# Infini-attention and GEGLU on one core: the hand-ordered main path replaced by one that a list scheduler orders at build time

## The chip, the cores and the metric

The kernel runs on one core of a Trainium2 chip. The metric is the device time of one execution in microseconds, as the median of several runs. The core has TensorE (PE, matrix multiplication), VectorE (DVE), ScalarE (ACT), GpSimd (POOL) and SyncE (SP, which issues most transfers). Each engine works through its own instructions in the order in which the program emits them, and waits for semaphores that other engines and transfers raise.

## The reference

The input is x, 2048 tokens of 448 features in bfloat16. Two branches share its layer norm, and the result is `x + s * silu(f)`.

```
xn = layernorm(x)
q, k, v = xn @ wq, xn @ wk, xn @ wv          # 16 heads of 28
for s in 4 segments of 512 tokens:            # per head
    a_dot = softmax(q k^T / sqrt(28) + causal mask) v
    a_mem = (phi(q) M) / (phi(q) z + 1e-6)    # phi(t) = t + 1 if t > 0 else exp(t)
    o     = g * a_mem + (1 - g) * a_dot       # g = sigmoid(beta)
    M, z += phi(k)^T v, sum phi(k)
s_out = o @ wo
f     = (gelu(xn @ w_gate) * (xn @ w_up)) @ w_down    # 448 -> 1792 -> 448
out   = x + s_out * silu(f)
```

## The kernel before

Work goes by segments of 512 tokens. The 448 features are cut into four chunks of 112 rows (`DC`), so that every matmul over features is four matmuls of 112 rows. The heads are padded from 28 to 32 columns and go in four groups of four, so that a group fills 128 partitions of `qT` and `kT`; column 28 of the padded v (`vaug`) is one and gives the softmax denominators.

The steps of a segment, with the lines that matter:

- **Layer norm** (L188 to L211): statistics and scaling on DVE, the power on POOL (L194), 16 transposes on PE (L204) and copies into `xnT`.
- **Projections** (`project_units`): q and k transposed, 512 columns wide (L253, casts L258 and L260), v by tokens (L275), and k once more by tokens (`ktok`, L283), from which phi(k) is formed for the memory update; phi(q) from L263 on.
- **Attention** (`attention`, `scores`, `pv`): 12 steps, three for each head group. A step has two half-steps of two heads. A half-step makes scores of two heads (L337, 32 rows each) into one of two score buffers in PSUM, exponentiates them on ACT (L341) and masks the diagonal blocks on POOL (L344). PV (L354) puts four heads into four column groups. `evac` (L364) copies the result and sends its denominators to DRAM (L366).
- **Reciprocals** (`invert`, L383 to L393): the denominators come back in another shape (`dc`), are inverted on DVE, go to DRAM (`rdr`, four transfers) and come back spread over partitions (`rb`, four transfers of 256 KB). `combine` (L408 to L411) scales on POOL and writes `oT`.
- **Memory** (`memory_read` L370, `update` L314 on).
- **Gate and up** (`gate_up`): 14 blocks of 128 columns; each has eight matmuls of 112 rows (L422), a Gelu on ACT (L425) and a product on DVE (L426). The blocks share the two score buffers in PSUM.
- **Down** (L437, 56 matmuls of 448 columns) and **finish** (L461 output projection, L464, L466 the residual on POOL, with x loaded once more as `xr`, L458).

The order is written by hand. For segments 0 to 2, gate and up of segment s come first, with tables that put layer norm, reciprocals and combining between its blocks. Attention of s follows, and `attention` fills the gaps between its half-steps with units of other work in proportion to costs written beside them: update, projections of s+1, down of s, finish of s-1. Segment 3 is the other way round: attention first, filled with down and finish of segment 2, then gate and up, then down and finish.

```
keyed.append(((c + u[0] / 2) / tot, n, u))     # merge(): units of several lists by share of cost
while fill and done < tot * n / (2 * len(steps)):   # attention(): fill after each half-step
```

Nearly all transfers are issued by SP in program order. PSUM holds two score buffers of two banks, one bank for PV and three for everything else.

Of the kernel before, what the change touches and what calls it, by code (L numbers as in the profile page):

```python
# [9 lines left out]
ALU = mybir.AluOpType  # L10
# [10 lines left out]
HG = 4  # L21
# [3 lines left out]

def fast_path(tc, A_x, A_wq, A_wk, A_wv, A_wo, A_beta, B_w_gate, B_w_up, B_w_down, out):
# [10 lines left out]
    DC = 112  # L37
    NDC = D // DC
    NFC = F // P
    RC = L // 64  # L40
    scale = float(Dh) ** -0.5

    with ExitStack() as ctx:
        pool = lambda name, bufs, **kw: ctx.enter_context(tc.tile_pool(name=name, bufs=bufs, **kw))
        const = pool("const", 1)
        xp = pool("xp", 2)
        xnp = pool("xnp", 2)
        seg1 = pool("seg1", 1)
        seg2 = pool("seg2", 2)
        work = pool("work", 2)  # L50
        ptp = pool("ptp", 6)
        oup = pool("oup", 4)
        rbp = pool("rbp", 4)
        blk = pool("blk", 5)
        small = pool("small", 4)
        dram = pool("dram", 2, space=DRAM)
        ps_s = pool("ps_s", 2, space=PSUM)
        ps_pv = pool("ps_pv", 1, space=PSUM)
        ps_m = pool("ps_m", 3, space=PSUM)
# [4 lines left out]
        def w_dma(eng, t, ap, rows):  # L64
            eng.dma_start(out=t[:], in_=ap.rearrange("(c p) n -> p c n", p=rows))

        x_sb = {}

        def load_x(s):
            x_sb[s] = xp.tile([P, NB, D], BF16, name="x_sb")  # L70
            for b in range(0, NB, 2):
                eng = nc.scalar if s == 0 and b else nc.sync
                eng.dma_start(out=x_sb[s][:, b:b + 2, :], in_=x_v[s][:, b:b + 2, :])

        load_x(0)
        ident = const.tile([P, P], BF16, name="ident")
        make_identity(nc, ident[:])
        nhalf = const.tile([P, NB], F32, name="nhalf")
        nc.gpsimd.memset(nhalf[:], -0.5)
        warm = const.tile([P, 1], F32, name="warm")  # L80
        nc.scalar.activation(out=warm[:], in_=nhalf[:, 0:1], func=ACT.Exp)

        wq_raw = seg2.tile([DC, NDC, D], BF16, name="oT")
        wk_raw = const.tile([DC, NDC, D], BF16, name="wk_raw")
        wv_sb = const.tile([DC, NDC, D], BF16, name="wv_sb")
        wg_sb = const.tile([DC, NDC, F], BF16, name="wg_sb")
        wu_sb = const.tile([DC, NDC, F], BF16, name="wu_sb")
        wd_sb = const.tile([P, NFC, D], BF16, name="wd_sb")
        wo_sb = const.tile([P, G, D], BF16, name="wo_sb")
        w_dma(nc.sync, wq_raw, A_wq, DC)  # L90
        w_dma(nc.scalar, wk_raw, A_wk, DC)
        w_dma(nc.sync, wv_sb, A_wv, DC)
        betac = const.tile([P, 1], A_beta.dtype, name="betac")
        nc.gpsimd.dma_start(
            out=betac[:],
            in_=A_beta.rearrange("(h o) -> h o", o=1).unsqueeze(1).to_broadcast([H, RC, 1]))
        w_dma(nc.sync, wg_sb, B_w_gate, DC)
        w_dma(nc.scalar, wu_sb, B_w_up, DC)
        load_x(1)
        w_dma(nc.sync, wd_sb, B_w_down, P)  # L100
        nc.gpsimd.memset(wo_sb[:], 0.0)
        wo_v = A_wo.rearrange("(g i d) n -> i d g n", i=HG, d=Dh)
        for i in range(HG):
            nc.sync.dma_start(out=wo_sb[i * HP:i * HP + Dh, :, :], in_=wo_v[i])

        raw = {"wq": wq_raw, "wk": wk_raw}
        wpad = {}
        for nm in ("wq", "wk"):
            wpad[nm] = const.tile([DC, NDC, H, HP], BF16, name=nm + "_pad")
            nc.gpsimd.memset(wpad[nm][:, :, :, Dh:HP], 0.0)  # L110

        def pad_weight(nm):
            nc.vector.tensor_copy(out=wpad[nm][:, :, :, 0:Dh],
                                  in_=raw[nm][:].rearrange("p c (h d) -> p c h d", d=Dh))

        bdmask = const.tile([P, P], F32, name="bdmask")
        vaug, pkb = [], []
        macc = const.tile([P, G, P], F32, name="macc")
        mbd = const.tile([P, G, P], BF16, name="mbd")
        igate = const.tile([P, 2], F32, name="igate")  # L120
        for i in range(2):
            vaug.append(const.tile([P, NB, H, HP], BF16, name=f"vaug{i}"))
            nc.gpsimd.memset(vaug[i][:, :, :, Dh:HP], 0.0)
            nc.gpsimd.memset(vaug[i][:, :, :, Dh:Dh + 1], 1.0)
        pkb.append(const.tile([P, NB, H, HP], BF16, name="pkb"))
        nc.gpsimd.memset(pkb[0][:, :, :, Dh:HP], 0.0)
        nc.gpsimd.memset(bdmask[:], 0.0)
        for i in range(HG):
            nc.gpsimd.memset(bdmask[i * HP:(i + 1) * HP, i * HP:(i + 1) * HP], 1.0)

        def gates():

            nc.scalar.activation(out=igate[:, 0:1], in_=betac[:], func=ACT.Exp)
            nc.scalar.activation(out=igate[:, 1:2], in_=betac[:], func=ACT.Exp, scale=-1.0)
            nc.vector.tensor_scalar(out=igate[:], in0=igate[:], scalar1=1.0, scalar2=2.0,
                                    op0=ALU.add, op1=ALU.mult)


        clock, waiting = [0], []

        def later(n, fn):
            waiting.append((clock[0] + n, len(waiting), fn))

        def tick():
            clock[0] += 1
            due = sorted(w for w in waiting if w[0] <= clock[0])
            waiting[:] = [w for w in waiting if w[0] > clock[0]]
            for _, _, fn in due:
                fn()

        oki = const.tile([1, 1], mybir.dt.int32, name="oki")

        def guard():
            sqs = {}
            for i, nm in enumerate(("wq", "wk")):
                sqs[nm] = oup.tile([DC, NDC, D], BF16, name=f"oU{i}")
                nc.scalar.activation(out=sqs[nm][:], in_=raw[nm][:], func=ACT.Square)
            ones = const.tile([P, 1], BF16, name="ones")
            nc.gpsimd.memset(ones[:], 1.0)
            nrm = small.tile([1, 2, H], F32, name="nrm")  # L160
            yield
            for i, nm in enumerate(("wq", "wk")):
                np_ = ps_m.tile([P, L], F32, name="m")
                for c in range(NDC):
                    nc.tensor.matmul(out=np_[0:1, 0:D], lhsT=ones[0:DC, :], rhs=sqs[nm][:, c, :],
                                     start=(c == 0), stop=(c == NDC - 1))
                nc.vector.reduce_sum(out=nrm[:, i, :],
                                     in_=np_[0:1, 0:D].rearrange("p (h d) -> p h d", d=Dh), axis=AX.X)
            okh = small.tile([1, H], F32, name="okh")
            nc.vector.tensor_tensor(out=okh[:], in0=nrm[:, 0, :], in1=nrm[:, 1, :], op=ALU.mult)  # L170
            nc.vector.tensor_scalar(out=okh[:], in0=okh[:], scalar1=(LOGIT_MAX / (D * scale)) ** 2,
                                    scalar2=None, op0=ALU.is_lt)
            nc.vector.tensor_reduce(out=oki[:], in_=okh[:], op=ALU.min, axis=AX.X)
            yield

        xnT = {}

        def layer_norm(s):

            xs = x_sb[s]  # L180
            xnT[s] = xnp.tile([DC, NDC, L], BF16, name="xnT")
# [782 lines left out]
```

## Time and profile before

| what | value |
| --- | --- |
| time, median of 3 runs | 335.21 us (335.02 to 335.26) |
| profiled execution, from first to last instruction | span 331.6 us |
| its own time outside the span | not recorded apart; the median is 3.6 us above the span |
| PE busy | 279.2 us, 84%, 1620 matmuls |
| DVE, ACT, POOL busy | 159.5, 152.0, 132.9 us |
| mean granted TensorE clock | 0.951 |
| read from and written to memory | 17.66 MB and 2.98 MB |
| instructions | 4480 |

A line of the profile names the line of the kernel, the engine, the operation, the tile that is written and those that are read, their shapes, the count, the busy time, the mean length of one, and the idle time of the engine ahead of it with what ended it. Busy time of PE is the union of matmuls that overlap in its pipeline, so a cost on PE is read from the distance between starts.

### The profile page before, as it was taken

To read this page: it belongs to the slowest core of one execution; us is meant where nothing else is said; L and a number is where in the kernel's file an instruction comes from. 1 tells how busy PE (TensorE), PEld (TensorE's weight loads), DVE (VectorE), ACT (ScalarE), POOL (GpSimd) and SP (SyncE) were. 2 spreads that over 40 slices of the span, in tenths; PEclk is the share of its full clock that TensorE was granted. 3 is DMA by queue.
4 is the path that set the end of the run, shared out by engine and by line. 5 is a ranking of instruction groups with operands and counts; after the bars stand their busy time and mean duration, and the time that the engine had idled before them with its cause. 6 is when DMAs were issued, how large, how long until landed. Compare 5 with 4: busy or idle time off the path is not lost.

```text
span 331.6 us, 4480 instructions
## 1 busy us (share of the span) xinstructions
PE 279.2 (84%) x1620; PEld 116.1 (35%) x1620; DVE 159.5 (48%) x301; ACT 152.0 (46%) x213; POOL 132.9 (40%) x219
## 2 busy tenths in 40 slices
PE   0699989999999999989999998198837973979691
PEld 0344434433334434333444432022312321434250
DVE  2447746645559567655585576145202531233221
ACT  1324542867772355556733386246643650223010
POOL 7000100333311245459410983286546743216712
PEclk9999999999999999999999999659996997799898
DMA  6998000000000520340102300510050021514011
GB/s 199 267 265 211 0 1 2 0 2 4 0 3 5 144 56 21 85 102 29 33 6 70 74 8 18 155 43 29 22 135 9 8 59 57 143 22 140 0 55 51
DMA packets 20773, 21.00 MB, mean 63 GB/s; under 512 B 6424, under 2 KB 16152, under 8 KB 20744
## 3 DMA queue, kind: packets, MB, share of 16 engines
q1 hardware_dynamic: 19512, 18.41, 21.3%
q10 hardware_dynamic: 1200, 2.24, 2.5%
q8 instruction: 14, 0.23, 0.3%
q14 instruction: 15, 0.12, 0.1%
q0 software_dynamic: 32, 0.00, 0.0%
HBM read 17.66 MB, written 2.98 MB: 62 GB/s over the span
## 4 chain that ended last, share of the span: by engine, by line
PE 54%; DMA 16%; POOL 11%; SPq 6%; DVE 5%; ACT 3%; issue 3%; POOLq 0%; DVEq 0%; ACTq 0%
PE s L422 21%; PE m L253 8%; PE m L437 7%; DMA xr<-in_A_x_dram 6%; PE s L337 5%; PE m L275 3%; DMA rdr<-dc 3%; POOL o_out L466 3%; POOL oU L410 3%; PE pv L354 3%; POOL oT L411 3%; PE m L283 3%; SPq L390 2%; SPq L393 2%; DMA oT<-in_A_wq_dram 2%
## 5 line engine op out<-in xcount | busy, mean ns | idle before, releaser
L341 ACT ACTIVATE pt<-s 128x1024 bf16<-128x1024 f32 (+1 forms) x96 | 81.6, 883 | 45.3 <-PE s L337 33.7
L344 POOL TENSOR_SCALAR_AFFINE_SELECT pt<-pt 128x256 bf16<-128x256 bf16 x128 | 51.7, 424 | 66.8 <-ACT pt L341 63.8
L425 ACT ACTIVATE gl<-s 128x512 bf16<-128x512 f32 x56 | 33.3, 597 | 75.1 <-PE s L422 75.0
L422 PE MATMUL s<-xnT,wg_sb 112*128 112x512 bf16 x224 | 58.9, 386 | 3.3 <-DVE hT L426 3.3
L426 DVE TENSOR_TENSOR hT<-gl,s 128x512 bf16<-128x512 bf16 x56 | 38.1, 683 | 49.2 <-ACT gl L425 49.1
L422 PE MATMUL s<-xnT,wu_sb 112*128 112x512 bf16 x224 | 58.4, 384 | 0.0
L437 PE MATMUL m<-wd_sb,hT 128*128 128x448 bf16 x224 | 51.8, 368 | 0.0
L354 PE MATMUL pv<-pt,vaug 128*32 128x512 bf16 (+3 forms) x256 | 21.2, 324 | 24.6 <-POOL pt L344 17.0
L337 PE MATMUL s<-qT,kT 32*128 32x128 bf16 (+3 forms) x256 | 33.1, 309 | 2.5 <-ACT pt L341 2.3
L466 POOL TENSOR_TENSOR o_out<-sg,xr 128x448 bf16<-128x448 f32 x16 | 16.9, 1059 | 41.0 <-DMA xr<-in_A_x_dram 31.4
L422 PEld LDWEIGHTS <-wu_sb 112*128 112x128 bf16 x224 | 22.1, 99 | 27.1 <-issue 1.3
L422 PEld LDWEIGHTS <-wg_sb 112*128 112x128 bf16 x224 | 21.1, 99 | 27.6 <-issue 6.4
L437 PEld LDWEIGHTS <-hT 128*128 128x128 bf16 x224 | 20.4, 101 | 22.6 <-issue 6.8
L194 POOL TENSOR_TENSOR rstd<-rstd,nhalf 128x2 f32<-128x2 f32 x8 | 5.8, 727 | 48.2 <-DVE rstd L192 48.1
L364 DVE COPY oU<-pv 128x512 f32<-128x512 f32 x16 | 11.0, 686 | 25.5 <-PE pv L354 15.3
L410 POOL TENSOR_TENSOR oU<-oU,rb 128x512 f32<-128x512 f32 x12 | 15.2, 1266 | 19.6 <-DMA rb<-rdr 19.6
L337 PEld LDWEIGHTS <-kT 32*128 32x128 bf16 x256 | 9.9, 92 | 37.2 <-issue 36.5
L446 DVE SCALAR_TENSOR_TENSOR sg<-th,m 128x448 f32<-128x448 f32 x16 | 9.9, 619 | 26.6 <-ACT th L441 24.4
L253 PE MATMUL m<-xnT,wq_pad 112*128 112x512 bf16 x64 | 19.1, 427 | 0.7 <-ACT xnT L209 0.7
L354 PEld LDWEIGHTS <-vaug 128*32 128x32 bf16 x256 | 6.5, 94 | 37.4 <-issue 34.2
L253 PE MATMUL m<-xnT,wk_pad 112*128 112x512 bf16 x64 | 18.6, 418 | 0.0
L461 PE MATMUL m<-wo_sb,oT 128*128 128x448 bf16 x64 | 16.0, 369 | 3.0 <-POOL oT L411 3.0
(76 smaller groups left out, 275.3 us busy)
## 6 DMA issues: line engine op xcount, KB each, us to landing
rb<-rdr SPq DMA_DIRECT2D x28, 256.0 KB
xr<-in_A_x_dram SPq DMA_DIRECT2D x16, 112.0 KB
out_dram<-o_out SPq DMA_DIRECT2D x16, 112.0 KB
x_sb<-in_A_x_dram SPq DMA_DIRECT2D x7, 224.0 KB
wu_sb<-in_B_w_up_dram ACTq DMA_DIRECT2D x1, 1568.0 KB
wg_sb<-in_B_w_gate_dram SPq DMA_DIRECT2D x1, 1568.0 KB
wd_sb<-in_B_w_down_dram SPq DMA_DIRECT2D x1, 1568.0 KB
rdr<-dc SPq DMA_DIRECT2D x28, 32.0 KB
```

The lines of the kernel that those rows point to most:

```text
L253: nc.tensor.matmul(out=pr[:], lhsT=wpad[nm][:, c, g * HG:(g + 1) * HG, :].rearrange("p h d -> p (h d)"), rhs=xnT[s][:, c, :], start=(c == ...
L337: nc.tensor.matmul(out=sp[:, j, c0:c0 + n], lhsT=kT[s][r, g, kb * P:(kb + 1) * P], rhs=qT[s][r, g, kb * P:L], start=True, stop=True)
L341: nc.scalar.activation(out=pt[:, :, 0:w], in_=sp[:, :, 0:w], func=ACT.Exp, scale=scale)
L344: nc.gpsimd.affine_select(out=v, in_=v, pattern=[[0, 2], [1, P]], compare_op=ALU.is_ge, fill=0.0, base=0, channel_multiplier=-1)
L354: nc.tensor.matmul(out=acc[i * HP:(i + 1) * HP, kb * P:L], lhsT=va[:, kb, g * HG + i, :], rhs=pts[i // 2][:, i % 2, c0:c0 + n], start=(kb ...
L410: nc.gpsimd.tensor_tensor(out=o_a[:], in0=o_a[:], in1=r[:], op=ALU.mult)
L422: nc.tensor.matmul(out=gu[:, i, :], lhsT=w_sb[:, c, fc * P:(fc + 1) * P], rhs=xnT[s][:, c, :], start=(c == 0), stop=(c == NDC - 1))
L425: nc.scalar.activation(out=gl[:], in_=gu[:, 0, :], func=ACT.Gelu_apprx_tanh)
L426: nc.vector.tensor_tensor(out=hT[s][:, fc, :], in0=gl[:], in1=gu[:, 1, :], op=ALU.mult)
L437: nc.tensor.matmul(out=d_ps[:, 0:D], lhsT=hT[s][:, fc, b * P:(b + 1) * P], rhs=wd_sb[:, fc, :], start=(fc == 0), stop=(fc == NFC - 1))
L461: nc.tensor.matmul(out=a_ps[:, 0:D], lhsT=oT[s][:, g, b * P:(b + 1) * P], rhs=wo_sb[:, g, :], start=(g == 0), stop=(g == G - 1))
L466: nc.gpsimd.tensor_tensor(out=o_out[:], in0=t[:], in1=xr[:], op=ALU.add)
```

## The change

The whole main path is written anew. Every piece of work becomes an `Op` with engine, an assumed occupation and latency, dependences, buffers and a priority; `arrange` goes through them with a list scheduler while the program is built, and the ops are emitted in the order of the start times that it assigns. What runs is still a fixed order on each engine with semaphores.

What else differs: attention has ten steps per segment instead of twelve, each with all four heads of a group, and with the short key blocks of two groups packed together; one step fills both score buffers. The 448 features are cut into three chunks of 128 rows and a remainder of 64. For gate and up, the remainders of gate (partitions 0 to 63) and up (64 to 127) lie in one tile, `wh_sb`, and are issued as neighbours for two blocks; the last chunk of `xnT` holds its 64 rows twice. Projections still take four matmuls, the remainder padded with zeros. `xnT` of segments 1 to 3 and phi(k) by tokens come from DMA transposes; k by tokens is no longer computed. x stays in SBUF for all four segments. phi works on two groups at a time, its min and max on POOL. Attention comes ahead of gate and up in every segment. PSUM has two score buffers and four other banks, which gate and up may use as well.

The diff, cut to its core ("-" lines are the code above and are left out):

```diff
+SEM, SWITCH, TABLE, AHEAD = 0.06, 0.1, 1.29, 0.2
+def arrange(ops):
...
+        t0, _, e0, _, _ = min(found, key=lambda c: c[:2])
+        s, _, e, o, picks = min((c for c in found if c[2] == e0 and c[0] <= t0 + AHEAD),
+                                key=lambda c: c[1])
+        occ, lat = o.eng[e]
+        if e == "PE" and o.mode and o.mode != mode:
+            s, mode = s + SWITCH, o.mode
...
+        o.start, o.on, o.done = s, e, s + lat
+        free[e] = s + occ
...
+    return sorted(done, key=lambda o: o.start)
...
+        S_ = banks(2, [P, 2, L], "s")
+        M_ = banks(4, [P, L], "m")
...
+        def dma(name, kb, fn, **kw):
+            return op(name, {"SP": (0.42, 2.0 + kb / 180)}, fn, **kw)
...
+        def warm_up():
+            for i in range(12):
+                nc.tensor.matmul(out=M_.aps[3], lhsT=warm[:, 0:P], rhs=warm[:], start=True, stop=True)
...
@@ layer_norm, s > 0 @@
+                for b in range(NB):
+                    o = dma(f"tr{s}{b}", 128, lambda b=b: nc.sync.dma_start_transpose(
+                        out=xT.ap()[:, :, b * P:(b + 1) * P], in_=xn.ap()[:, b, :]),
...
@@ phi @@
+                o = act(f"ex{nm}{s}{half}", 2 * L, lambda: nc.scalar.activation(
+                    out=e.ap(), in_=src[0].ap()[:, gs, :], func=ACT.Exp), func="exp",
...
+                o = gps(f"mi{nm}{s}{half}", 1.0, lambda: nc.gpsimd.tensor_scalar(
+                    out=e.ap(), in0=e.ap(), scalar1=1.0, scalar2=0.0, op0=ALU.min, op1=ALU.max),
...
+                        pk[s][1].append(dma(f"tk{s}{g}", 128, lambda j=j, g=g:
+                            nc.sync.dma_start_transpose(out=dst.ap()[:, g], in_=e.ap()[:, j, :]),
...
+        def steps_of(g0, g1):
+            return [[(g0, 0, 0)], [(g0, 1, 0), (g0, 3, 384)], [(g0, 2, 0), (g1, 2, 256)],
+                    [(g1, 0, 0)], [(g1, 1, 0), (g1, 3, 384)]]
...
@@ attention, scores of one step @@
+                    for g, kb, c0 in st:
+                        n = L - kb * P
+                        for i in range(HG):
+                            r = slice(i * HP, (i + 1) * HP)
+                            nc.tensor.matmul(out=S2[i // 2].ap()[:, i % 2, c0:c0 + n],
+                                             lhsT=kT[s][0].ap()[r, g, kb * P:(kb + 1) * P],
+                                             rhs=qT[s][0].ap()[r, g, kb * P:L], start=True, stop=True)
...
+                for pr in range(2):
+                    x = act(f"ex{s}{k}{pr}", 2 * L, lambda pr=pr: nc.scalar.activation(
+                        out=pt.ap()[:, 2 * pr:2 * pr + 2, :], in_=S2[pr].ap(), func=ACT.Exp,
...
@@ gate_up, two blocks @@
+                def halves(fc=fc, bank=bank):
+                    for j in range(2):
+                        for i in range(2):
+                            r = slice(i * HALF, (i + 1) * HALF)
+                            nc.tensor.matmul(out=bank(j, i), lhsT=wh_sb[r, (fc + j) * P:(fc + j + 1) * P],
+                                             rhs=xT.ap()[r, NC3, :], start=True, stop=False)
...
+        for s in range(NSEG):
+            if s == 0:
+                layer_norm(1, at(A(0), -100))
+            attention(s, A(s))
+            if s > 0:
+                read(s, at(A(s), 0))
+            if s < LAST:
+                update(s, at(A(s), 10))
...
+            gate_up(s, Gp(s), tabled)
+            tabled = []
+            combine(s, at(Gp(s), -500))
...
+            if s + 2 <= LAST:
+                layer_norm(s + 2, at(Gp(s), 100))
...
+        for b in range(NB):
+            down(LAST, b, at(8, 10 * b))
+            finish(LAST, b, at(8, 10 * b + 5))
...
+        with tc.manual_schedule():
+            for o in arrange(ops):
+                if o.fn is not None:
+                    o.fn()
```

More of the change, by code (lines that the diff above doesn't have):

```diff
@@ L116, in fast_path @@
[L116 to L125, printed above, removed]
```

1124 lines of the change are left out of this document (683 added, 441 removed).

## The prediction

> **What bounds the kernel now.** I read the page first: the busy tenths in 40 slices, with the granted clock below.
>
> ```profile
> PE   0699989999999999989999998198837973979691
> PEclk9999999999999999999999999659996997799898
> ```
>
> TensorE (PE) is full from the third slice to about 200 us; after that it has holes and a lowered clock. Then the stretches between stage limits, taken from the timeline: start, gate/up 0, attention 0, gate/up 1, attention 1, gate/up 2, and all after that (segment 3). Columns are length, then busy time of each engine with instruction counts, then clock and DMA.
>
> ```profile
> core 0: us, PE busy (x) PEld busy (x) DVE busy (x) ACT busy (x) POOL busy (x), PEclk, DMA share, GB/s
> 0.00:29.60 29.60, 18.19 (x81) 8.69 (x82) 12.85 (x29) 7.70 (x13) 6.80 (x23) 1.00 0.97 249
> 29.60:58.40 28.80, 27.41 (x140) 12.58 (x139) 17.35 (x39) 12.82 (x18) 1.50 (x3) 1.00 0.07 16
> 58.40:95.00 36.60, 36.60 (x252) 14.26 (x253) 20.60 (x38) 27.20 (x40) 13.35 (x33) 1.00 0.01 2
> 122.50:163.40 40.90, 39.93 (x266) 15.93 (x267) 25.04 (x44) 26.20 (x36) 23.83 (x41) 1.00 0.21 55
> 189.90:331.60 141.70, 103.43 (x598) 40.23 (x595) 49.43 (x81) 56.69 (x77) 71.75 (x105) 0.88 0.21 56
> ```
>
> Segments 0 to 2 are bound by PE: less time there needs less PE work. Segment 3 is bound by waits: PE idles 38.3 of 141.7 us. The waits view names one of them, POOL behind reloads of x:
>
> ```profile
> POOL o_out L466 <- DMA xr<-in_A_x_dram: 31.4, 10, 9.6
> ```
>
> Next, durations by shape, then PE's timeline at an ordinary attention step and at one in segment 3 (start, length, instruction, count).
>
> ```profile
> L341 ACT ACTIVATE pt<-s 128x1024 bf16<-128x1024 f32 x64 | 63.4, 1025 | 28.8 <-PE s L337 18.5 <-POOL o_out L466 8.6 <-POOL pt L344 1.7
> L344 POOL TENSOR_SCALAR_AFFINE_SELECT pt<-pt 128x256 bf16<-128x256 bf16 x128 | 51.7, 424 | 66.8 <-ACT pt L341 63.8 <-DMA den<-oU 2.5
> L283 PE MATMUL m<-wk_raw,xnT 112*128 112x448 bf16 x48 | 10.6, 354 | 0.1
> ...
> 67.30 0.39 PE L337 MATMUL s<-qT,kT 32*128 32x512 bf16 x2
> 67.61 0.40 PE L354 MATMUL pv<-pt,vaug 128*32 128x384 bf16 x8
> 67.95 1.12 PE L437 MATMUL m<-wd_sb,hT 128*128 128x448 bf16 x5
> 69.00 0.39 PE L337 MATMUL s<-qT,kT 32*128 32x512 bf16 x2
> ...
> 255.31 0.40 PE L337 MATMUL s<-qT,kT 32*128 32x512 bf16 x6
> 255.64 0.29 PE L354 MATMUL pv<-pt,vaug 128*32 128x256 bf16 x4
> ```
>
> Starts, not lengths, give the cost, since matmuls overlap. A full 512-column matmul takes 0.216 us (gate/up chunks of eight start 1.73 apart), so 0.213 is streaming; one of 448 takes 0.189. Five of 448 should take 0.945 and take 1.05 (67.95 to 69.00): leaving for a 32-row form costs 0.105. Two scores of 512 take 0.31: together 0.213, plus 0.10 for the next change of form. The six at 255.31 are 2,048 columns in 0.33 us: four 32-row groups run at once (one after another would be 0.85).
>
> **The change, part by part.** PE work of one segment, in us.
>
> *Gate/up.* Now 14 x 8 x 0.216 = 24.2. Then per two blocks: four 64-row matmuls in two pairs (2 x 0.213), 12 full ones (2.59), two changes of form (0.21) = 3.23, times 7 = 22.6. That the two 64-row groups run together no row shows. Bounds: as the 32-row groups do (22.6), or one after the other (+0.43 x 7 = 25.6). I take 22.6, the nearest row being the four-group one.
>
> *Scores and PV.* Now 24 score groups of two heads: 10,240 columns at two at once (4.3) and two changes each (5.1), and 12 PV groups (2.1 + 12 x 0.12), about 13. Then 10 steps of four heads: 10 x (0.105 + 0.213 + 0.105 + 0.213 + 0.125) = 7.6. On ACT the 24 exps (16 of 1025, 8 of 601 ns, 20.6 busy) become 20 of 1025, 19.8 at the 0.99 busy each that the row gives. The masks on POOL stay 32 x 0.424.
>
> The Trainium skill (TensorE: Matmul & The Clock Gate, Measured speedup vs the span model) measured 3.07 times for four row groups, not 4. By that the scores would stream 2.8 us a segment instead of 2.1 and the sum would be 2.6 us higher; the 0.33 us for six matmuls speaks for 4.
>
> *Removed from PE.* The token-major k matmuls, 16 x 0.189 = 3.0 in segments 0 to 2, and the 16 LayerNorm transposes of each of segments 1 to 3 (L204: 64 busy for 7.1 us, so 1.8 a segment). They become 24 DMA transposes of 128 KB on SP's queue, and phi(k) is taken from kT.
>
> *The transposes' price.* No row has one. Below: a plain load of like size, xr (112 KB), lands in 2.0 us and holds SP for 0.43; the POOL and DVE work around them is kept off PE, so no gain beyond that PE time. Above: if it went in 32-byte pieces, 4,096 packets at 58 ns each (21.3% of 16 x 331.6 us over 19,512 packets of q1) on 16 engines: 14.8 us. I take 2.5, nearest to the like-sized load. xnT is needed a whole stage later, so this is hidden; what waits behind them in SP's queue are the den, dc, rdr and rb transfers and the stores. If the cover is gone, PE stalls at the projection, and once more at update.
>
> The Trainium skill (VectorE: DVE Perf Modes, The three transpose paths) puts a 128x128 DMA transpose at 1309 ns against 390 on TensorE, which speaks against this edit; an estimate from it is 5.2 us per transpose, 42 per segment on the queue, and the sum of the third rival below. No run here shows it yet.
>
> *x kept on chip* removes 16 reloads and POOL's 31.4 us behind them; in segments 1 and 2 PE was full all the same, so the gain counts in segment 3.
>
> *The order.* Now gate/up(s) precedes attention(s). Then attention(s) comes first, with down and output projection of s-1 and projection of s+1 between its steps, then gate/up(s), and at the end only down and output projection of segment 3. So attention 3 has PE fill and the reciprocal chain (den, dc, rdr, rb, about 20 us) runs beside 22.6 us of gate/up. What it adds: one step's scores fill both score buffers, so the next step's first complete exp often waits for both exps. A row's price for that turn: scores start 240.19, exp 240.68, 0.49, against zero where the second head pair alone is late; I take 0.45.
>
> The stages then, each the larger of PE and ACT plus what their coupling loses:
>
> - Start to first exp: x lands at 4.1; four blocks of statistics, scaling and copies fill DVE for 6.5; transpose and copy 1.3; two projections 1.73; cast and scores 1.0: 14.6.
> - Attention 0: PE 7.6 + 9.9 (projection) + 1.0 (update) is less than ACT: 19.8 + 6 phi exps (6.0) + 10 x 0.45 = 30.3.
> - Attention 1: PE 7.6 + 9.9 + 10.6 (down, 56 x 0.189) + 3.0 + 1.0 + 0.9 = 33.0; ACT 19.8 + 4.0 + 2.2 (tanh) + 4.5 + 1.3 (table) = 31.8. So near each other they lose some: 36. Attention 2, two phi exps fewer: 35.5.
> - Attention 3: PE 22; ACT 19.8 + 2.2 + 4.5 + 1.3 = 27.8: 28.5.
> - Gate/up: 4 x 22.6 = 90.4. Eight handovers at 0.5: 4.
> - Down and output projection: 13.6. From PE's end: tanh, two products and a DVE add (now POOL's 1.03) 2.8, and 3.9 from the last store's issue to the end as now: 6.7.
>
> Sum: 14.6 + 130.3 + 90.4 + 4 + 13.6 + 6.7 = 259.6. The profiled span is 331.6 and the median 335.2, so 3.6 lies outside it: **263 us**. By stages, the gain is mostly segment 3's: after gate/up 2 the rest takes 142 us now, and 28.5 + 22.6 + 13.6 + 6.7, with handovers about 72, then.
>
> **Rivals.**
> - *Lock-step (0.20).* PE works in a fixed order; if it reaches the scores inside a fill block (up to 1.05), every step costs 2.0 of exp, 0.6 of other ACT work, 0.5 turn and 1.0 of late arrival: 41, 41, 36 and 33 us for the four attentions instead of 130.3, 151 in all. For: both score buffers go at once, and ACT and PE are 1 us apart. Against: today's PE is full in attention 0. Time: 284.
> - *The pairing does nothing (0.06).* The 64-row halves run one after the other, so this part of the change does not do what it says: +0.43 x 28 = 12, 275.
> - *Transposes somewhat late (0.07).* At 5 us each, between the bounds, the four before a projection take 10 us longer than forecast; the stage before hides some 6, the rest is a stall, three times: 275.
> - *Transposes very slow (0.06), slower than before.* At 14.8 us each, 24 hold SP's queue for 355 us, and everything else in it comes on top: about 370. It decides from about 7 us, where eight per segment no longer fit beside the rest of the queue in a 57 us segment, and makes the kernel slower from about 10: (335 - 263) / 24 = 3 us beyond those 7. For: 16,152 of 20,773 packets of now are under 2 KB, so small pieces do happen. Against: a plain load of the size takes 2.0.
>
> **How the numbers follow.** The forecast has 0.60 (its own range 250 to 276), the rivals 0.20, 0.06, 0.07, 0.06, and 0.01 is left for no change that can be told: about 0.2%, 0.7 us, is what a measurement of this kernel can tell. Low end: no turn and no coupling loss, attentions 26 + 33 + 33 + 24, 14 less, and half the handovers: 247. High end: lock-step with transposes a few us late, 292. Faster 0.93, same 0.01, slower 0.06.
>
> **What would show it.** Right: gate/up pairs 3.2 us apart; scores of a one-part step 0.33 apart; PE at 8 tenths or more to the last slices, clock whole; ACT's exps 2.4 us per step in attention 0; transposes landing near 2.5 us; SP's queue far from full. Wrong: ACT's idle time before L341's successor above 1 us per step (lock-step); pairs 3.7 apart (no pairing); PE waiting for xnT (transposes). The forecast falls if PE idles over 60 us in all.

## The result: 290.4 us, faster, but 27 us short of the forecast

The changed kernel takes 290.44 us (289.36 to 291.33, four runs) beside 335.12 us for the kernel before on the same chip: 0.8688 of it, 95% interval 0.8639 to 0.8737. The gain is 44.7 us where 72 was forecast. The profiled execution took 290.03 us with a span of 288.3, so 1.7 us lie outside the span, not 3.6. Medians count every execution; where some ran at a lower clock, in the second group of experiments above all, the ratio uses the others alone and so is not the quotient of the medians.

The page of the changed kernel: PE's busy tenths and clock in 40 slices of 7.2 us, then two groups (busy, mean ns, idle time ahead).

```profile
PE   7893029889997999599769999989697999998991
PEclk9996557999999999999979999999999999999998
...
L682 ACT ACTIVATE pt<-s 128x1024 bf16<-128x1024 f32 x80 | 77.5, 1022 | 34.5 <-PE s L670 33.3
...
L638 DVE TENSOR_TENSOR oa<-oa,rb 128x512 f32<-128x512 f32 x12 | 13.6, 1169 | 9.2 <-DMA rb<-rdr 9.2
```

The holes that PE had after 200 us are gone: the last half is at 9 tenths nearly throughout. There are new ones: a deep one in the fourth to sixth slice, with the clock down to half, one in the twentieth and twenty-first, and one at 5 tenths in the seventeenth (115 to 122 us, in attention 1), to which the open points come back. The windows put the first two at 20 to 50 and at 140 to 150 us (length, busy us and instructions of each engine, then granted clock, DMA share, GB/s):

```profile
core 0: us, PE busy (x) PEld busy (x) DVE busy (x) ACT busy (x) POOL busy (x), PEclk, DMA share, GB/s
20.00:30.00 10.00, 3.97 (x40) 1.23 (x37) 2.34 (x3) 7.47 (x10) 8.04 (x16) 0.68 1.13 271
30.00:40.00 10.00, 0.00 (x0) 0.00 (x0) 7.11 (x19) 0.00 (x0) 0.00 (x0) 0.50 0.60 82
40.00:50.00 10.00, 8.85 (x60) 3.76 (x60) 4.71 (x10) 3.81 (x4) 2.19 (x5) 0.63 0.18 37
140.00:150.00 10.00, 5.52 (x19) 1.69 (x18) 7.02 (x8) 1.79 (x3) 5.72 (x4) 0.83 0.32 77
```

From 30 to 40 us PE, ACT and POOL do nothing at all; only DVE works. The waits view (total us, times, longest) names what came last for each hole:

```profile
PE m L450 <- DMA xnT<-xn: 14.4, 1, 14.4
...
DVE st L365 <- DMA x_sb<-in_A_x_dram: 11.1, 2, 10.2
DVE oa L638 <- DMA rb<-rdr: 9.2, 6, 4.3
PE m L765 <- DVE hT L785: 8.0, 4, 4.5
```

Stage by stage, us. A is attention, G gate/up. G starts at its first gate/up matmul, and the next A at the first other matmul behind the last of them; the last eight PV matmuls of attentions 0 and 3 so fall into G0 and G3 of the changed kernel. The best experiment is the one with the transposes of segment 1 back on PE, below.

| | first score | A0 | G0 | A1 | G1 | A2 | G2 | A3 | G3 | down, output | tail |
|---|---|---|---|---|---|---|---|---|---|---|---|
| forecast, 0.5 of handover in each A and G | 14.6 | 30.8 | 23.1 | 36.5 | 23.1 | 36.0 | 23.1 | 29.0 | 23.1 | 13.6 | 6.7 |
| changed kernel | 15.5 | 45.7 | 24.1 | 40.3 | 29.0 | 35.6 | 25.7 | 27.4 | 25.3 | 13.8 | 6.0 |
| best experiment | 15.8 | 34.0 | 26.7 | 32.7 | 22.5 | 35.7 | 22.5 | 28.9 | 25.2 | 13.8 | 5.9 |

Against the first row A0 is 14.9 us over, A1 3.8, the four gate/ups together 11.7 and the start 0.9; down and output add 0.2, and A2, A3 and the tail give 2.7 back. That is, but for rounding, the 28.7 us by which the span is longer than the forecast sum.

### The profile page after: what moved, and what is told of

The parts are those of the page before. It is cut to its first block, busy times and chain, and to the rows that moved or that the text cites. A ratio compares the mean times of both kernels' runs of the same rounds, so it can differ in the third digit from the quotient of the medians.

```text
span 288.3 us, 4343 instructions
## 1 busy us (share of the span) xinstructions
PE 241.7 (84%) x1562; PEld 100.5 (35%) x1562; DVE 173.2 (60%) x286; ACT 147.3 (51%) x183; POOL 129.2 (45%) x210
## 5 line engine op out<-in xcount | busy, mean ns | idle before, releaser
L682 ACT ACTIVATE pt<-s 128x1024 bf16<-128x1024 f32 x80 | 77.5, 1022 | 34.5 <-PE s L670 33.3
L802 PE MATMUL m<-wd_sb,hT 128*128 128x448 bf16 x224 | 46.6, 353 | 0.5 <-DVE qT L460 0.3
L450 PE MATMUL m<-xnT,wq_pad 128*128 128x512 bf16 (+1 forms) x80 | 17.5, 349 | 14.4 <-DMA xnT<-xn 14.4
L785 DVE TENSOR_TENSOR hT<-gl,s 128x512 bf16<-128x512 bf16 x31 | 20.3, 677 | 13.3 <-ACT gl L781 13.3
L781 ACT ACTIVATE gl<-m 128x512 bf16<-128x512 f32 x25 | 14.9, 597 | 20.5 <-PE m L775 17.3
L775 PE MATMUL s<-xnT,wg_sb 128*128 128x512 bf16 x93 | 25.3, 381 | 0.0
L775 PE MATMUL s<-xnT,wu_sb 128*128 128x512 bf16 x93 | 25.1, 379 | 0.0
L670 PE MATMUL s<-qT,kT 32*128 32x512 bf16 (+3 forms) x256 | 19.4, 307 | 5.9 <-ACT pt L682 5.6
L729 PE MATMUL m<-pt,vaug 128*32 128x128 bf16 (+3 forms) x256 | 18.6, 315 | 3.6 <-POOL pt L694 3.4
L775 PE MATMUL m<-xnT,wg_sb 128*128 128x512 bf16 x75 | 21.0, 391 | 0.0
L775 PE MATMUL m<-xnT,wu_sb 128*128 128x512 bf16 x75 | 20.7, 385 | 0.0
L638 DVE TENSOR_TENSOR oa<-oa,rb 128x512 f32<-128x512 f32 x12 | 13.6, 1169 | 9.2 <-DMA rb<-rdr 9.2
L450 PE MATMUL m<-xnT,wk_pad 128*128 128x512 bf16 (+1 forms) x80 | 17.4, 348 | 0.0
```

The lines of the kernel that those rows point to most:

```text
L450: nc.tensor.matmul(out=bank.ap()[:, lo:hi], lhsT=wpad[nm][:, c, g * HG:(g + 1) * HG, :].rearrange("p h d -> p (h d)"), rhs=xT.ap()[:, c, l ...
L638: o = dve(f"ca{s}{g}", 0.6, lambda t=t, r=r: nc.vector.tensor_tensor(out=t.ap(), in0=t.ap(), in1=r.ap(), op=ALU.mult), deps=[o, ro], prio= ...
L670: nc.tensor.matmul(out=S2[i // 2].ap()[:, i % 2, c0:c0 + n], lhsT=kT[s][0].ap()[r, g, kb * P:(kb + 1) * P], rhs=qT[s][0].ap()[r, g, kb * P ...
L682: x = act(f"ex{s}{k}{pr}", 2 * L, lambda pr=pr: nc.scalar.activation(out=pt.ap()[:, 2 * pr:2 * pr + 2, :], in_=S2[pr].ap(), func=ACT.Exp, ...
L729: nc.tensor.matmul(out=acc[g].ap()[i * HP:(i + 1) * HP, kb * P:L], lhsT=va[s][0].ap()[:, kb, g * HG + i, :], rhs=pts[kk][0].ap()[:, i, c0: ...
L775: nc.tensor.matmul(out=bank(j, i), lhsT=w[:, c, (fc + j) * P:(fc + j + 1) * P], rhs=xT.ap()[:, c, :], start=False, stop=(c == NC3 - 1))
```

## The experiments

Each ran beside the kernel before on its own chip (median 334.31, 335.02 and 334.34 us in the three groups), which is what the ratios are against. In the second group (wo late, both weights late, the combine on POOL, and all of these together) the kernel before scattered from 329.78 to 335.97 us, so their intervals are wide. Since the order is made by `arrange`, an edit to an assumed time or an engine can also move other work; where that shows, it is said.

### The hole in attention 0

DVE's and SP's timelines of the changed kernel (start, length, instruction, count, idle ahead). SPq rows are SP's issues, and their length is the time that SP was held:

```profile
12.31 11.84 SPq L318 DMA_DIRECT2D wo_sb<-in_A_wo_dram  x4
24.20 0.40 SPq L320 DMA_DIRECT2D x_sb<-in_A_x_dram  x1
24.70 5.03 SPq L512 DMA_TRANSPOSE pk<-e  x2
34.64 5.12 SPq L419 DMA_TRANSPOSE xnT<-xn  x4
```

```profile
32.51 0.63 DVE L365 BATCH_NORM_STATS2 st<-x_sb 128x6 f32<-128x448 bf16 x1 [10.16 <-DMA x_sb<-in_A_x_dram]
33.05 1.30 DVE L387 TENSOR_SCALAR xn<-x_sb,mv,rs 128x448 bf16<-128x448 bf16 x4
...
41.15 1.86 PE L450 MATMUL m<-xnT,wq_pad 128*128 128x512 bf16 x4 [14.41 <-DMA xnT<-xn]
```

Read from the bottom. PE's projection of segment 1 waits for segment 1's transposes. They wait for four scalings of 0.33 us on DVE. These stand in DVE's order behind a statistic of segment **3**, which waits 10.16 us for x of segment 3. That x was issued at 24.20, because the four loads of wo ahead of it held SP for 11.84 us. The plan had 0.42 us for each of these issues and had x landing 12 us after its own. Theory: the wait goes in pieces, as x, wo and w_down are taken out of the transposes' way. Rival: the transposes themselves are slow.

**x of segment 3 loaded earlier, the plan's order kept.**

```diff
+        nc.sync.dma_start(out=xs[3][:], in_=x_v[3])      # behind x of segment 1
-        x_in[3] = [op("x3", {"SP": (0.42, 12.0)}, lambda: nc.sync.dma_start(out=xs[3][:], in_=x_v[3]),
-                      after=wo_in, prio=0)] * NB
+        x_in[3] = [op("x3", {"SP": (0.42, 12.0)}, None, after=wo_in, prio=0)] * NB
```

> The changed kernel with one transfer moved: x of segment 3 is issued right behind x of segment 1 instead of behind wo; the order on every compute engine is unchanged. Theory (DVE stands at the statistics of segment 3's x, 22.3 to 32.5 us, and the scaling of segment 1 is queued behind them): the 14.4 us wait of PE for xnT goes, and with it some 2.5 us of half clock behind it; span 288 to about 272, time about 274. Rival (the DMA transposes or the full DMA engines make xnT late): the wait stays above 8 us, because x arrives no sooner on SP's queue than the transposes leave it; time 283 to 290.

Measured: 284.98 us, ratio 0.8537 (0.8477 to 0.8597), 5.5 less than the changed kernel. DVE's wait is gone, but PE's is not. The timelines of this run:

```profile
13.57 11.65 SPq L319 DMA_DIRECT2D wo_sb<-in_A_wo_dram  x4
...
28.03 6.75 SPq L419 DMA_TRANSPOSE xnT<-xn  x4
...
36.15 0.58 PE L450 MATMUL m<-xnT,wq_pad 128*128 128x512 bf16 x1 [9.15 <-DMA xnT<-xn]
```

SP is still held by wo until 25.2, and the pair of phi(k) transposes goes first. The theory is right in part, 5.3 of the 14.4 us; the time and the 9.15 us that are left lie where the rival had put them.

**The plan told the truth about x.** The loads stay; `x3` is said to land after 27 us instead of 12, so that `arrange` puts segment 3's statistics later.

```diff
-        x_in[3] = [op("x3", {"SP": (0.42, 12.0)}, lambda: ...
+        x_in[3] = [op("x3", {"SP": (0.42, 27.0)}, lambda: ...
```

> The changed kernel with one number of the scheduler changed: it is told that x of segment 3 lands 27 us after its issue instead of 12; no transfer moves. Theory: segment 3's statistics go behind segment 1's scaling on DVE and the PE wait for xnT falls from 14.4 to under 3 us; time 273 to 278. Rival (transposes or DMA load): the wait stays, 283 to 290.

Measured: 283.83 us, ratio 0.851 (0.8458 to 0.8562): 6.6 us for one number. PE's wait for xnT is 7.9 us, not under 3, so this too ends in the rival's range. Here the order moved elsewhere too: A1 fell to 34.9 while G0 rose to 26.1.

**wo behind segment 1's transposes**, with x early:

```diff
+                wo_in[0].after += [xnT[1][1][-1], pk[0][1][-1]]
+                for n in range(1, HG):
+                    wo_in[n].after.append(wo_in[n - 1])
```

> As x3_early, and the four loads of wo are issued behind segment 1's transposes and phi(k)'s, so SP is free from about 13.5 us instead of 25.3; the order on the compute engines is the same. Theory (SP's queue, held 11.7 us by wo's four issues, makes the transposes late): the 9.15 us wait of PE that x3_early left falls to under 3 us; time about 277. Rival (the transposes wait in the DMA rings behind the weights, w_down above all, which land until about 30 us): the wait falls by under 3 us; time 282 to 285.

Measured: 280.95 us, ratio 0.8517 (0.8343 to 0.8691). PE's wait for xnT falls by 2.05 us to 7.10, not to under 3 as the theory had it; the rival had a fall of under 3.

**w_down behind them as well**: its load becomes an op, and wo follows it.

```diff
-        nc.sync.dma_start(out=wd_sb[:], in_=B_w_down.rearrange("(c p) n -> p c n", p=P))
+        wd_in = op("wd", {"SP": (0.42, 12.0)}, lambda: nc.sync.dma_start(
+            out=wd_sb[:], in_=B_w_down.rearrange("(c p) n -> p c n", p=P)), prio=0)
+                wd_in.after += [xnT[1][1][-1], pk[0][1][-1]]
+                wo_in[0].after.append(wd_in)
```

> As wo_late, and w_down too is issued behind the transposes. SP's queue alone is at fault: the same as wo_late. The rings' backlog is at fault: the wait that wo_late leaves falls here to under 2 us; time 274 to 277. Either way, if the wait goes and the time does not, the reading of attention 0 is wrong.

Measured: 280.95 us, ratio 0.8508 (0.8343 to 0.8672). The two times can't be told apart, but the traces differ: PE's wait for xnT falls from 9.15 to 7.10 with wo late and to 5.77 with w_down late too, where a backlog of the weights as the only cause would have left under 2. A0 falls from 45.7 (changed kernel) over 40.4 (x early) and 37.3 to 36.4. Neither theory held alone. With SP free and the scalings done, the last 5.8 us are the transposes' own way. In the version with both weights late and the combine on POOL (below), they look like this:

```profile
26.44 5.12 SPq L420 DMA_TRANSPOSE xnT<-xn  x4
...
32.90 1.86 PE L451 MATMUL m<-xnT,wq_pad 128*128 128x512 bf16 x4 [5.77 <-DMA xnT<-xn]
```

Four issues of 1.28 us and 1.3 to land: 6.5 us from first issue to first use. This is far cheaper than the 10 us that I took for four, but it lies on the path.

### The waits in gate/up

The hole at 140 us, in DVE's and PE's timelines of the changed kernel:

```profile
136.05 0.69 DVE L785 TENSOR_TENSOR hT<-gl,s 128x512 bf16<-128x512 bf16 x1 [0.61 <-ACT gl L781]
141.08 0.69 DVE L638 TENSOR_TENSOR oa<-oa,rb 128x512 f32<-128x512 f32 x1 [4.34 <-DMA rb<-rdr]
142.05 3.94 DVE L638 TENSOR_TENSOR oa<-oa,rb 128x512 f32<-128x512 f32 x3 [0.28 <-DMA rb<-rdr]
145.92 1.27 DVE L785 TENSOR_TENSOR hT<-gl,m 128x512 bf16<-128x512 bf16 x2
...
146.65 1.18 PE L765 MATMUL m<-xnT,wh_sb 64*128 64x512 bf16 x3 [4.48 <-DVE hT L785]
```

The combine's first product (L638, `oa` times the reciprocals in `rb`) is put on DVE by the change, and waits 4.3 us for rb. The products `hT` stand behind it although their inputs are there; PSUM banks are not freed, and PE stops for 4.48 us. The four products themselves then hold DVE until 145.99, another 4.9 us.

**The combine's first product on POOL** (segments 0 to 2).

```diff
-                    o = dve(f"ca{s}{g}", 0.6, lambda t=t, r=r: nc.vector.tensor_tensor(
+                    e, t_ = (gps, 1.27) if s < LAST else (dve, 0.6)
+                    o = e(f"ca{s}{g}", t_, lambda t=t, r=r: (nc.gpsimd if s < LAST else nc.vector).tensor_tensor(
```

> The changed kernel with the first product of combine (oa x rb) on POOL instead of DVE for segments 1 and 2; nothing else. Theory (DVE stands at these products, waiting for rb, and gate/up's products are queued behind them): PE's waits of 4.48 and 2.61 us in gate/up 1 and 2 go, with 1.5 us of half clock behind the first; gate/up 1 and 2 take 23 to 24.5 instead of 29.0 and 25.7 us, time 283 to 285. Rival (DVE has too much to do in gate/up whatever it waits for): gate/up 1 stays above 27.

Measured: 277.52 us, ratio 0.8381 (0.8209 to 0.8552): 12.9 less than the changed kernel, more than expected. G1 goes from 29.0 to 22.53 and G2 from 25.7 to 22.54, which is the forecast's PE work of 22.6; G0 and A0 give 0.9 and 1.1. The waits of this run show the same late rb, now in front of an engine on which nothing urgent is queued:

```profile
POOL oa L639 <- DMA rb<-rdr: 24.1, 2, 13.2
...
PE m L766 <- DVE hT L786: 0.8, 1, 0.8
```

The edit takes the wait and the products' own time off DVE together, so it does not separate the two. The run with unpaired halves (below) keeps the products on DVE but waits for rb at most 1.0 us, and there PE's stop in G1 is 0.33 us, which speaks for the wait as the larger part.

**Both weights late, x early and the combine on POOL.**

> wd_wo_late and combine_pool together. Theory (two separate head-of-line waits): the gains add, 7 us under wd_wo_late, 267 to 270. Rival (a later start of gate/up is what made rb late, so an earlier schedule has no second wait): as wd_wo_late within 2 us.

Measured: 271.08 us, ratio 0.8191 (0.8036 to 0.8346). The gain over the changed kernel is 19.4 us, of 22.4 if the two added in full; A0 is 36.1, G1 and G2 are 22.54, and 1.5 us are lost in A3.

### What the pairing is worth

**Both remainders on the same 64 rows**, in the changed kernel: the four matmuls can't share the array.

```diff
-        wh_sb = const.tile([P, F], BF16, name="wh_sb")
+        wh_sb = const.tile([HALF, 2, F], BF16, name="wh_sb")
-                            nc.tensor.matmul(out=bank(j, i), lhsT=wh_sb[r, (fc + j) * P:(fc + j + 1) * P],
-                                             rhs=xT.ap()[r, NC3, :], start=True, stop=False)
+                            nc.tensor.matmul(out=bank(j, i), lhsT=wh_sb[:, i, (fc + j) * P:(fc + j + 1) * P],
+                                             rhs=xT.ap()[0:HALF, NC3, :], start=True, stop=False)
```

The loads follow, and the tile `rb` has four buffers instead of six, to make room. So the time holds that change too; the rows of PE below do not.

> The changed kernel with both 64-row remainders, of gate and of up, on partitions 0 to 63 (two fewer rb buffers make room; the planned order is the same). Theory (the pair runs at once, so the pairing saves 0.43 us per two blocks): the four 64-row matmuls take 0.96 instead of 0.54 us, 28 times, +12 us, time about 301, a little less where DVE makes PE wait anyway. Rival (the pair gains nothing): no change, 289 to 292.

Measured: 290.25 us, ratio 0.8685 (0.8626 to 0.8744), the same as the changed kernel. And yet PE's rows did what was expected. First the changed kernel, then this one:

```profile
65.73 0.61 PE L765 MATMUL m<-xnT,wh_sb 64*128 64x512 bf16 x4
66.27 0.82 PE L775 MATMUL m<-xnT,wg_sb 128*128 128x512 bf16 x3
...
68.96 0.60 PE L765 MATMUL s<-xnT,wh_sb 64*128 64x512 bf16 x4
```

```profile
190.71 1.03 PE L764 MATMUL m<-xnT,wh_sb 64*128 64x512 bf16 x4
191.67 0.82 PE L774 MATMUL m<-xnT,wg_sb 128*128 128x512 bf16 x3
```

Four halves take 0.54 us from start to next start when paired and 0.96 when not. What takes most of it up is the wait of the section before: PE's stop for `hT` falls from 4.48 to 0.33 us in G1 and from 2.61 to nothing in G2. A slower PE reaches the wait when it is nearly over. G1 even gets shorter (26.4 for 29.0 us) and G2 stays (25.55 for 25.7), while G0 and G3 are longer by 2.6 and 0.8; A0 gives 2.1 back, which the pairing does not explain. That the wait hides the pairing is a theory that can be tried: without the wait, the pairing must show.

**The same edit on the version with both weights late and the combine on POOL.**

> wd_wo_late_combine_pool with both 64-row remainders on partitions 0 to 63, as in halves_single. Theory (the pairing's gain was swallowed by DVE's wait for rb in gate/up; with that wait gone it counts in full in gate/up 1 and 2, and less in 3): gate/up 1 and 2 go from 22.5 to 25.6 us each, the whole 8 to 12 us slower than 271, 279 to 283. Rival (something else sets gate/up's length): within 2 us of 271.

Measured: 280.2 us, ratio 0.8399 (0.834 to 0.8458), 9.1 more than the 271.08 with the pairing. G1 and G2 go from 22.54 to 25.55, which is 7 times 0.43, so the gain shows in full where the wait is gone. G0 takes 2.6 more and G3, which keeps its combine on DVE, only 0.9.

### x kept on chip alone

The kernel before, with `xp` of four buffers, `blk` of four and `small` of two, and no reload:

```diff
-                xr = work.tile([P, D], BF16, name="xr")
-                nc.sync.dma_start(out=xr[:], in_=x_v[s][:, b, :])
-                nc.gpsimd.tensor_tensor(out=o_out[:], in0=t[:], in1=xr[:], op=ALU.add)
+                nc.gpsimd.tensor_tensor(out=o_out[:], in0=t[:], in1=x_sb[s][:, b, :], op=ALU.add)
```

> The kernel before, with x of all four segments kept on chip and the 16 reloads (xr) left out; one buffer fewer for sg and two fewer for small tiles. My prediction's reading (the reloads count in segment 3 alone, where 11 of them make POOL wait): between 4 and 20 us faster, 315 to 331; the chain's 6% for xr would be 20. Rival (the wait only moves, to the reciprocal chain that ends at about the same time): within 3 us of 335.

Measured: 312.41 us, ratio 0.9357 (0.9305 to 0.9408): 21.9 us from a few lines, more than expected, and half of the whole change's gain. The span is 310.7 instead of 331.6. Gate/up 2 ends at 188.7 instead of 189.9, so 19.7 of the 20.9 us are in segment 3, where the forecast had put them. It had given them no size.

### The port between DVE and POOL

In the changed kernel two of phi's twelve `scalar_tensor_tensor` are long, 3.84 us at 118.39 (in attention 1) and 3.75 at 184.26, where the others take 1.2 to 1.5, and the twelve float32 products of the combine take 1.17 on average where the shortest take 0.68. So I measured DVE's operations by themselves, four of each: alone, beside 16 masks of POOL, and beside six float32 additions of POOL, all appended to the changed kernel and run once.

> The changed kernel with a measurement behind its last store: on DVE four each of phi's scalar_tensor_tensor (1024 bf16), the f32 product of combine (512), a cast out of PSUM (512) and phi's min/max (1024 bf16); first alone, then beside 16 masks on POOL, then beside 6 f32 additions on POOL. Theory (a DVE instruction with two SBUF operands and POOL shut each other out): scalar_tensor_tensor 1.21 alone and over 2 us, up to 3.8, beside masks; the f32 product 0.68 alone and 1.1 to 1.75 beside additions; the PSUM cast 0.68 in every case. Rival (POOL's masks slow everything on DVE alike, or the long one of 118 us was a wait that the trace hides): no difference between the kinds beyond 20%.

| four of DVE's | alone | beside masks: DVE, and POOL's 16 | beside additions: DVE, and POOL's 6 |
|---|---|---|---|
| scalar_tensor_tensor, bf16, 1024 | 4.99 | 5.18, 9.55 | not measured |
| product, f32, 512 | 2.86 | 3.05, 7.49 | 5.62, 9.26 |
| cast from PSUM, 512 | 2.86 | 2.80, 5.81 | 2.80, 7.96 |
| min and max, bf16, 1024 | 1.80 | 1.99, 10.62 (not all of it beside, see below) | 4.56, 8.20 |

The rows of DVE beside nothing, then POOL's last masks, and the last group of `scalar_tensor_tensor` with the additions that were meant to run beside it:

```profile
284.85 4.99 DVE L921 SCALAR_TENSOR_TENSOR e<-qT,e 128x1024 bf16<-128x1024 bf16 x4
...
322.29 10.62 POOL L936 TENSOR_SCALAR_AFFINE_SELECT pt<-pt 128x256 bf16<-128x256 bf16 x16 [0.59 <-DVE pt L943]
...
324.59 5.17 DVE L921 SCALAR_TENSOR_TENSOR e<-qT,e 128x1024 bf16<-128x1024 bf16 x4
...
332.88 7.96 POOL L950 TENSOR_TENSOR om<-om,om 128x512 f32<-128x512 f32 x6
```

DVE had finished that group 3 us before POOL's additions began, so the `scalar_tensor_tensor` was never beside them. It ran beside the masks that were left of the group before, and these make up most of the 10.62 us: the four masks beside min and max took 0.47 to 0.59 us.

The expectation missed in part: the `scalar_tensor_tensor` was to stretch to 2 to 3.8 us beside masks, and it did not. Beside masks it is POOL that loses: a mask takes 0.41 us beside the cast, up to 0.59 beside min and max, 0.85 beside the product and 1.39 beside the `scalar_tensor_tensor`. DVE loses beside POOL's float32 additions, in its float32 product and its min and max, by about 2 and 2.5 times. A cast from PSUM is not slowed by either.

What the long one waited for stands in the changed kernel's own trace:

```profile
118.31 0.41 POOL L694 TENSOR_SCALAR_AFFINE_SELECT pt<-pt 128x256 bf16<-128x256 bf16 x1
118.68 1.03 POOL L827 TENSOR_TENSOR oo<-sg,x_sb 128x448 bf16<-128x448 f32 x1
119.67 1.48 POOL L694 TENSOR_SCALAR_AFFINE_SELECT pt<-pt 128x256 bf16<-128x256 bf16 x4
...
118.39 3.84 DVE L506 SCALAR_TENSOR_TENSOR e<-kT,e 128x1024 bf16<-128x1024 bf16 x1 [1.55 <-POOL e L490]
```

DVE's operation began 0.08 us after a mask, POOL ran six operations without a gap at their usual length, and DVE's ended 1.08 us after the last of them, a little less than the 1.2 us that it needs by itself. Every one of phi's operations over 2 us, in the traces of the changed kernel and its versions, ends 1.07 or 1.08 us after such a run. So DVE stood until POOL's unbroken run was over. In other places POOL's operation is the one that is held (a mask of 1.39 us beside DVE's 1.40 at 170.85); what decides between them no run here shows.

### The transposes of segment 1 back on PE

On the version with both weights late and the combine on POOL, segment 1's xnT is made as segment 0's is: 16 transposes on PE into banks of `M_`, and four copies on ACT.

```diff
-            if s == 0:
+            if s <= 1:
-                    tp = Buf((S_, 1))
+                    tp = Buf((S_ if s == 0 else M_, 1))
```

> wd_wo_late_combine_pool with segment 1's xnT made by 16 PE transposes and ACT copies, as segment 0's, instead of 4 DMA transposes. Theory (what is left of the wait in attention 0, 5.77 us plus half clock behind it, is the price of the DMA transposes, 1.25 us each on SP's queue against 0.42 planned): the wait falls under 1.5 us, 5 to 8 us faster, 263 to 266. Rival (the four score steps queued behind would only move the wait to update and phi(k)'s transposes): within 2 us of 271.

Measured: **265.21 us** (264.28 to 265.58), ratio 0.7928 (0.7878 to 0.7977), the fastest of all: 5.9 below the same version with DMA transposes, 25.2 below the changed kernel, 69 below the kernel before. PE no longer waits for xnT. A0 falls from 36.1 to 34.0 and A1 from 39.3 to 32.7, while G0 takes 2.6 more and A3 is the same. A0 and G0 together thus take 60.7 us for 60.2: the 5.77 us of waiting went into the transposes themselves, work that moved there, and new waits of PE (2.1 us in A0, 1.8 in G0). All of the gain is in A1, and it came by the plan: DVE has 28 operations in A1 instead of 37 and 38 in G0 instead of 33 (four copies of `om` among those that moved, with the four matmuls of the memory read that they copy), and PE's waits of 1.7 to 1.9 us for DVE's `om` and `sg` in A1 are gone. The page's ACT row shows how little the exps still wait:

```profile
L685 ACT ACTIVATE pt<-s 128x1024 bf16<-128x1024 f32 x80 | 77.5, 1023 | 16.7 <-PE s L673 15.5
```

**phi's min and max on DVE**, on top of that (0.65 us in the plan instead of 1.0 on POOL).

```diff
-                o = gps(f"mi{nm}{s}{half}", 1.0, lambda: nc.gpsimd.tensor_scalar(
+                o = dve(f"mi{nm}{s}{half}", 0.65, lambda: nc.vector.tensor_scalar(
```

> fixes_pe_transposes1 with phi's min and max on DVE (about 0.65 us each) instead of POOL (1.04). Theory (attention 1 is 3.7 us longer than attention 2 because DVE's scalar_tensor_tensor stands 3.84 us behind POOL's masks and additions; less work on POOL leaves it gaps): attention 1 falls from 39.3 to 36 to 37, 2 to 4 us faster than fixes_pe_transposes1. Rival (DVE, the busier of the two, takes the load worse): the same or up to 4 us slower.

Measured: 268.89 us, ratio 0.8035 (0.7982 to 0.8087): 3.7 slower. A0 and G0 together take 64.4 instead of 60.7; in G0 PE waits up to 2.57 us for `hT`. In this plan the quicker operation on the engine that frees PSUM costs more than the slower one on POOL. The long operations were gone (at most 1.44 us), and A1 was no shorter for it, 34.5 us for 32.7.

## Why the prediction was right and wrong

**The sign and the range held**, 290 in 247 to 292, but the forecast's own range, 250 to 276, was missed. That 290 still lies inside is luck: the upper end was made of lock-step and slightly late transposes. It was not lock-step. That rival made ACT's exps arrive late in every step and every attention dearer; but A3 took 27.4 where lock-step had 33 and the forecast, handover included, 29.0. ACT's wait for scores, whose sign was above 1 us per step, was 33.3 us for 40 steps, and 15.1 of that is the one hole in A0. (The rival was also priced some 10 us too low: ten steps of 2.0, 0.5 and 1.0 alone are 35 us, so its 36 and 33 for A2 and A3 do not follow from its own terms.) The turn of 0.45 us per step was sized about right: ACT's waits for scores in the best version are 15.5 us for 40 steps, 0.39 each, all else included. Of the other signs, PE idled 46.6 us, under the 60 at which the forecast falls; PE waiting for xnT did come.

**The PE work was right.** Paired blocks come 3.23 us apart (65.73 to 68.96), as worked out, and unpaired halves cost 0.42 more, as the rival "the pairing does nothing" had it (0.43); this rival is settled by the rows above and by the 9.1 us. Its 12 us was an upper end, since G3 hardly felt the difference. The scores of a one-part step start 0.33 before what follows:

```profile
89.08 0.39 PE L670 MATMUL s<-qT,kT 32*128 32x512 bf16 x4
89.41 2.82 PE L802 MATMUL m<-wd_sb,hT 128*128 128x448 bf16 x14
```

Down and output projection took 13.8 (13.6), the tail 6.0 (6.7).

**The first step that failed is a cover: "xnT is needed a whole stage later, so this is hidden".** That is so for segments 2 and 3: PE waits for xnT once in the whole kernel. Segment 1's xnT is made at the start and wanted inside attention 0, in the stage in which it is made. I wrote the order down ("projection of s+1 between its steps") and did not ask what work hides the transposes in the first segment. What came last there changed three times as each cause was taken away. Of the 14.41 us, x of segment 3 in front on DVE was 5.3 (to 9.15), wo in front on SP 2.0 (to 7.10), w_down 1.3 (to 5.77), and the transposes' own time the last 5.8, which went only when they left the DMA. These are shares of the wait, from one trace each. The stages followed as long as the DMA did the transposing (A0 45.7, 40.4, 37.3, 36.4 us); with the transposes on PE the wait went, but A0 and G0 together did not get shorter.

The warning stood in the trace of before. This row of SP's timeline, which I had not shown, says that four small loads hold SP for 16 us:

```profile
8.63 15.95 SPq L104 DMA_DIRECT2D wo_sb<-in_A_wo_dram  x4
```

I counted what stands behind the transposes in SP's queue, and not what stands ahead of them.

**Their price was not the fault.** I took 2.5 us each, and SP was held 1.3 in the four of segment 1, these being usable 6.5 us after the first issue. Only the first transposes of phi(k), while weights still streamed, were dearer: 2.96 us for one in the changed kernel, 3.87 with wo late. The third and fourth rivals (5 and 14.8 us) fall. By the Trainium skill (VectorE: DVE Perf Modes, The three transpose paths) the estimate was 5.2 us per transpose; the trace has a quarter of that on the queue. Its ranking, TensorE ahead of DMA, is not settled here: the swap in segment 1 came with 5.9 us less, but these are in A1, where the plan had changed, and for the other segments no run shows it.

**The second step that failed is a term that is missing**: the gate/ups at 22.6 and eight handovers at 0.5. The diff moves the combine's first product to DVE, and I priced the reciprocal chain as running "beside 22.6 us of gate/up". It does, but DVE's place in line waits for it, with `hT` behind it and PE behind that: 6.4 us in G1, 3.2 in G2, shown by moving that product alone, its own time on DVE included. I had listed what queues behind SP's transfers, but not what queues behind DVE's. In G1 and G2 this wait also swallowed the pairing's gain, as the pair of runs with and without the wait shows.

**x kept on chip** was put in the right place and not sized: 21.9 us alone. So the kernel before, with no more than that, was at 312, and everything else in the change bought 22 more.

**What stays open.** A1 took 40.3 us for 36.5 forecast. It is 32.7 in the best version, under the forecast, so no fixed cost is behind it, but how much each wait there was worth is not separated. The long operation alone does not explain it: the best version has one of 3.86 us in its A1 as well. Around the changed kernel's seventeenth slice PE waited 1.4 us for masks and 1.9 for `sg`, which stood behind the long operation on DVE. G3 keeps 2.6 us over its PE work in the best version; the last eight PV matmuls of attention 3 fall into it, and PE waits 1.1 us for `hT` there. Its combine stayed on DVE, and POOL was not tried for it. The best version's span of 263.6 is 4 us above the forecast sum, with A0 and G0 together 6.8 over and A1 3.8 under: the sum described the kernel without those two waits well, in part because these two offset each other.

## What to carry to other kernels

A list scheduler's order is only as good as the times it is told, and on an engine that works in order one operation that waits for a far transfer holds everything behind it: look in the plan for operations with a transfer among their inputs, and ask what stands behind each. Ask a "hidden" claim of the first segment and the last one separately. And a saving that measures as nothing may be a saving that a wait has taken; remove the wait, then measure it again.

## What the runs showed of the hardware

- Four loads of wo (98 KB each) held SP for 11.84 us in the changed kernel, 10.55 of them for the first of the four, while 303 GB/s were moved, and for 15.95 us in the kernel before, at 265 GB/s. Issued after the weights, the same four took 1.68 us in the run with wo late (79 GB/s), and 2.92 us right behind w_down (194 GB/s). An issue is not always the 0.4 us that x of segment 3 took at 24.20.
- After 14 us without work, PE had a granted clock of 0.50 while the projection's four matmuls at 41.15 ran: 1.79 us to the next start, where four of them take 0.96 at a clock of 1.00 (37.08 to 38.04 in the run with wo and w_down late).
- DVE and POOL hold each other up. Beside POOL's masks, DVE's operations were hardly slowed in the run by themselves (5.18 us for 4.99, 3.05 for 2.86) and the masks took up to 1.39 us for 0.41 beside the cast; beside POOL's float32 additions, DVE's float32 product doubled (5.62 for 2.86). In the changed kernel DVE lost to masks too: its operation at 118.39 ended 1.08 us after POOL's unbroken run of five masks and an addition.
